# A list of operations that begins at slot 10 of the first layer instead of slot 28

## The chip, the cores and the metric

The kernel runs on one core of one Trainium2 chip. The metric is the device time of one execution in microseconds, from the first to the last thing that the program does there. Five engines work beside each other, each through its own instructions in order: TensorE (PE in the profile, its weight loads PEld), VectorE (DVE), ScalarE (ACT), GpSimd (POOL) and SyncE (SP), which here issues every transfer between the device memory and the core's SBUF. TensorE writes its results into eight banks of PSUM.

## The reference

Three steps, all in float32. First a retention (an attention without softmax, with a decay): for 4 batches, 8 heads, 576 positions and 64 values a head, the scores q k^T / 8 are multiplied by gamma^(i - j) for j <= i and by 0 otherwise, and by v. The result is one matrix x of 2304 tokens by 512 values. Then two layers of the same shape:

```
h = x @ w_in            # 512 -> 2048
g = h * cos(h)          # second layer: 0 for h <= -1, h for h >= 1, (h + 1)^2 / 4 between
x = g @ w_out           # 2048 -> 512
```

## The kernel before

**Numbers in two parts.** Every operand of a product is kept as a high and a low part (fp32r), and a product is made of three: high by high, the weight's low by high, the weight's high by low. The weights come as raw 64-bit words and are converted on the chip.

**Tokens and slots.** The tokens stand in five blocks, the first of 256 and four of 512 (`BLOCKS`, line 25). The 2048 hidden values stand in 16 parts. A slot is one block with one part; `slots` (from line 556) lists the 80 of them, the first two blocks interleaved (slots 0 to 31), then blocks 2, 3 and 4 with 16 slots each. A slot of block 0 is narrow (256 columns), the others are wide (512). Slot s has a first product (`mm1`, step m: h = x w_in, 12 matmuls), a chain that makes g of h, and a second product (`mm2`, step M, 12 matmuls into banks that gather the output). The chain is, in order: h, a copy out of PSUM (tile hs; blocks 0 and 1 alone), a (turns, ScalarE), A (rounded, VectorE), b (cosine, two steps of ScalarE), C (times h, VectorE), g (the high part gh, ScalarE), G (the low part gl, GpSimd). The first product has two PSUM banks in turn, so that of slot s + 2 needs the copy of slot s. The second product of a slot stands two slots behind its first (`LAG` = 2).

**The first layer's weights** (wi0 to wi15, wo0 to wo15) are converted on the way (`Conversion`): each needs a raw load and, for most, the same words again shifted by two bytes (tiles raw and rsh, two homes of each); then X (ScalarE, reads raw), C (VectorE, reads rsh), W (VectorE, two steps), O (ScalarE, the high part) and M (VectorE, the low part). The converted wi are also stored (`store1`, wd) and loaded again for blocks 2 to 4.

**The second layer's weights** are prepared in the background from slot 28 (`bg0`) on, in 32 pieces (`piece`): a raw load, X, W and two more steps, a high part and a low part in a home of the wi ring (tile cw), stores of it; each second piece also makes sums of two pieces, which are rounded (tile tw) and stored in four parts. The second layer loads all of these as tiles w from wq and wv; its first product of all (bkT<-xc,w) reads the first of them.

**What sets the order.** The opening is a list written by hand (`OPENING`), kept as it is on every engine. Then, before the change, a plain loop issues slots 10 to 27, whose order the compiler's scheduler chooses. From slot 28 on the order comes from a planner: `op` notes for each operation its engine, a cost (`COST`), a place in time, what it reads and what it writes, and `listed` goes through them with one clock for each engine: of the operations that are ready it takes the one whose place is earliest; TensorE's stand in the order noted; one of SP can't start before its place. The order found is kept on every engine, and what the planner took for time is not used on the chip. The second layer's list follows behind the first layer's on every engine, SP too.

Of the kernel before, what the change touches and what calls it, by code (L numbers as in the profile page):

```python
# [14 lines left out]
ALU = mybir.AluOpType  # L15
# [35 lines left out]
E1 = 5.75  # L51
PACE = 9.0
BG_AT = 0.0
BEHIND = 8.0
LATS = (0.12, 0.2)
COST = dict(turn=0.58, psum1=0.68, cos=1.3, copy4=0.65, low4=0.69, low2=0.42, copy2=0.42, copy8=1.06, low8=1.23, masks=1.12, state=1.1, high=0.75, scores=1.0, w8=0.86, nothing=0.02, PE=1.04, mm2=2.72, psum=0.556, wide=0.96, copy=0.85, square=0.9, evac=0.68, pool=2.15, load=0.06)
# [53 lines left out]
a:8 b:7 A:8 g:6 W:wo4 m:9 b:8 G:6 M:5 h:9 M:wo4 a:9 C:7 A:9 M:6 g:7 C:8 O:wo4 G:7 g:8 b:9 G:8 M:7 C:9 g:9 G:9 M:8  # L110
low:8 store:5
# [4 lines left out]
def retention_moe_kernel(ctx: ExitStack, tc: tile.TileContext, qk, kv, win1, wout1, win2, wout2, ktab, out):  # L116
# [656 lines left out]
    for _ in range(2):  # L773
        load_raw(0, *queue.pop(0))
# [98 lines left out]
    def listed(lat):  # L873
        waits = [len(o[4]) for o in ops]
        users = [[] for _ in ops]
        for n, o in enumerate(ops):
            for x, lands in o[4]:
                users[x].append((n, lands))
        ready = [o[2] if o[0] == "SP" or not o[4] else 0.0 for o in ops]
        free = dict(PE=0.0, ACT=0.0, DVE=0.0, POOL=0.0, SP=-60.0)  # L880
        queue = {e: {n for n, o in enumerate(ops) if o[0] == e and (e == "PE" or not waits[n])} for e in free}
        order = []
        while len(order) < len(ops):
            best = None
            for e, ns in queue.items():
                if e == "PE":
                    n = min(ns, default=None)
                    if n is None or waits[n]:
                        continue
                elif ns:  # L890
                    t1 = min(max(free[e], ready[n]) for n in ns) + 0.15
                    n = min((n for n in ns if max(free[e], ready[n]) <= t1), key=lambda n: (ops[n][2], n))
                else:
                    continue
                t = max(free[e], ready[n])
                if best is None or t < best[0]:
                    best = t, n
            t, n = best
            e, cost = ops[n][:2]
            queue[e].remove(n)  # L900
            free[e] = t + cost
            order.append((t, n))
            for u, lands in users[n]:
                ready[u] = max(ready[u], t + cost + (0.0 if not lands or ops[u][0] == e else 6.0 if e == "SP" else lat))
                waits[u] -= 1
                if not waits[u] and ops[u][0] != "PE":
                    queue[ops[u][0]].add(u)
        return order

    loop_end = bg0  # L910
    for s in range(bg0):
        if s == 24:
            by_hand[0] = 0
        steps_of(s, "m")
        if s >= 1:
            steps_of(s - 1, "CgG")
        steps_of(s, "haA")

        todo = [x for x in jobs.get(s, []) if x not in opened]
        begun = [begin(0, *x) for x in todo]  # L920
        for x in todo:
            begun.pop(0).rest(home1(*x))
            if queue:
                load_raw(0, *queue.pop(0))
        for x in todo:
            if x[0] == 0:
                store1(x[1])
        if s >= LAG:
            steps_of(s - LAG, "M")
            evac(s - LAG)  # L930
        steps_of(s, "b")

    def when(s):
        return (s - bg0) * E1

    def first_layer_ops():
        LOW = "DVE"
# [6 lines left out]
        def retention(i, k, g, e):  # L944
# [16 lines left out]
            def at_load():  # L961
                op("SP", "load", t0 - 17, lambda: load(0), (), (q,))
                op("SP", "load", t0 - 16, lambda: load(1), (), (v,))
# [8 lines left out]
            def at_attend():  # L972
                op("PE", "scores", t0 + E1, go("attend", *(() if last else ("state",))), (q, v, ("T",), ("R",)), banks)
                if CHUNKS[i][1] == 0:
                    op("ACT", "high", t0 + E1 + 1, go("add_state"), banks, (("T",),))
                elif not last:
                    op("DVE", "state", t0 + E1 + 1, go("add_state"), banks, (("T",),))
                op("ACT", "high", t0 + E1 + 2, go("high"), banks, (("xh", l),))
                opened_by.append(op("DVE", "w8", t0 + E1 + 3, go("low"), (*banks, ("xh", l)), (("xl", l),)))
# [20 lines left out]
        def wi_place(s):  # L1000
            return ("cw", 1) if s == bg0 else ("wi", s % 3)

        def chain(s, which="aAbCgG"):
            b, h, t, j = when(s), bank_of(s), ("t", s % 3), (N1 - 1 - s) % (LAG + 1)
            hi, lo = ("gh", j), ("gl", j)
            for x in which:
                eng, cost, pos, reads, writes = dict(
                    a=("ACT", "turn", 2.8, (h,), (t,)), A=("DVE", "psum1", 3.7, (h,), (t,)), b=("ACT", "cos", 5.0, (), (t,)),
                    C=("DVE", "psum1", 6.5, (h,), (t,)), g=("ACT", "copy4", 8.0, (t,), (hi,)), G=(LOW, "low4", 9.0, (t, hi), (lo,)))[x]
                op(eng, cost, b + pos, lambda x=x: steps_of(s, x), reads, writes)  # L1010

        def second(s):
            l, c = slots[s]
            j = (N1 - 1 - s) % (LAG + 1)
            op("PE", "mm2", 0, lambda: steps_of(s, "M"), (("gh", j), ("gl", j)), keys_y(l) if c in (0, NC - 1) else ())
            if c == NC - 1:
                o, n = BLOCKS[l]
                per = 512 // n
                for e, y in enumerate(keys_y(l)):
                    eng = ("ACT", "DVE")[e >= 2]  # L1020
                    opened_by.append(op(eng, "copy4", when(s + LAG) - 5, lambda e=e, eng=eng: evac(s, only=e, eng=eng), (y,)))


        dp = PACE
        prev = {}

        def piece(j):
            i, c = bg[j]
            p = j * dp + BG_AT
            raw, X, W, cw = ("raw", j % 3), ("X", j % 2), ("W", j % 2), ("cw", j % 2)  # L1030
# [33 lines left out]
            op("SP", "load", p - 10, lambda: load_raw(1, i, c), (), (raw,))  # L1064
# [4 lines left out]
            op("DVE", "low4", p + 3, joined, (X, W), (("V", 0), ("V", 1)) if not two_of_it else (v,))  # L1069
# [4 lines left out]
            for a, b in pieces:  # L1074
                op("SP", "load", p + 6, lambda a=a, b=b: store(a, b), (cw,))
# [33 lines left out]
            for k, a in enumerate(((5, 4, 7, 6), (5, 7, 4, 6))[i]):  # L1109
                op("SP", "load", p + 9, lambda k=k, a=a: store_sum(k, a), (("tw",),))  # L1110

        chain(bg0 - 1, "CgG")
        done_pieces = 0
        for s in range(bg0, N1):
            for fn in plan.pop(2 * s, []):
                fn()
            if s >= pos_of[2, 0]:
                op("SP", "load", when(s) - 13, lambda s=s: load_wi(slots[s][1]), (), (wi_place(s),))
            l = slots[s][0]
            op("PE", "mm2", 0, lambda s=s: steps_of(s, "m"), (wi_place(s), ("xh", l), ("xl", l)), (bank_of(s),))  # L1120
# [3 lines left out]
            second(s - LAG)  # L1124
            while done_pieces < len(bg) and done_pieces * dp + BG_AT <= when(s + 1):
# [339 lines left out]
```

## Time and profile before

| | us |
|---|---|
| three runs | 820.22, 818.06, 821.0 (median 820.22) |
| the profiled execution | 818.65 |
| its span, first to last instruction | 816.9 |
| TensorE busy | 805.4 |
| VectorE busy | 635.1 |
| ScalarE busy | 542.7 |
| GpSimd busy | 126.2 |

The opening takes about the first 77 us of the span; slots 10 to 27 come next; the list of the first layer goes on to 456 us; the second layer takes the rest. In the profile L133 is the line through which the ordered part of the program issues, so the tiles' names tell what an operation is: h and hs belong to the first product, gh and gl to the chain's end, bky, bkS and bkO to the second product, X, W, C, raw, rsh, wi, wo to a conversion, cw, tw and V to the second layer's pieces. A matmul's duration includes the filling of the array, so that the starts of two neighbours lie closer than a duration.

### The profile page before, as it was taken

Reading aid. Unit: us, or ns where it says so; the run is one execution under the profiler, and the core shown is the slowest. Engines: PE = TensorE matmul, PEld = TensorE weight load, DVE = VectorE, ACT = ScalarE, POOL = GpSimd, SP = SyncE. Lnnn points to the kernel's source line nnn. Section 1 sums busy time; section 2 is a strip of 40 time slices with the busy share of each in tenths; the row PEclk is TensorE's granted clock in tenths of the full one; section 3 lists DMA queues with packets and bytes.
Section 4 is the critical chain, followed back from the end, with each engine's and each line's share of the span. In section 5 each row is a group of like instructions: output and inputs, shape, how many; then the busy total and the mean of one; then the engine's idle time right before and its main releaser. Section 6 shows DMA issues by size and latency. Waiting matters only on the chain.

```text
span 816.9 us, 14708 instructions
## 1 busy us (share of the span) xinstructions
PE 805.4 (99%) x5549; PEld 728.2 (89%) x5550; DVE 635.1 (78%) x956; ACT 542.7 (66%) x890; POOL 126.2 (15%) x99
## 2 busy tenths in 40 slices
PE   8999999999999999999999999999999999999997
PEld 6888789888878888888888899999999999999997
DVE  7988878697898877887896377886777885974675
ACT  4778788765556656666765578786666786576671
POOL 2333222222122222232232100000000000000000
PEclk9999999999999999999999999999999999999999
DMA  9997999399777998688976699888899888888883
GB/s 358 396 388 281 357 321 336 133 354 346 272 276 260 338 327 275 228 303 279 340 238 230 203 336 293 291 250 253 254 333 325 251 254 255 272 307 253 254 256 127
DMA packets 78006, 232.92 MB, mean 285 GB/s; under 512 B 8304, under 2 KB 15088, under 8 KB 77936
## 3 DMA queue, kind: packets, MB, share of 16 engines
q1 hardware_dynamic: 77936, 231.98, 82.7%
q8 instruction: 44, 0.72, 0.3%
q14 instruction: 26, 0.21, 0.1%
HBM read 184.76 MB, written 47.19 MB: 284 GB/s over the span
## 4 chain that ended last, share of the span: by engine, by line
PE 90%; DMA 4%; DVE 2%; ACT 2%; issue 1%; SPq 0%; POOL 0%; DVEq 0%; ACTq 0%; POOLq 0%
PE bkT L133 42%; PE bky L133 21%; PE h L133 19%; PE bkS L133 4%; PE bkO L133 4%; DMA rsh<-in_wout_dram 2%; DMA qkv<-in_qk_dram 1%; PE h L580 1%; DMA qkv<-in_kv_dram 1%; DMA raw<-in_wout_dram 1%; ACT t L133 1%; DVE t L133 0%; ACT gh L133 0%; DVE wo L133 0%; DVE X L133 0%
## 5 line engine op out<-in xcount | busy, mean ns | idle before, releaser
L133 PE MATMUL h<-xhl,wi 128*128 128x512 f32 (+1 forms) x816 | 180.7, 370 | 2.2 <-ACT hs L133 1.8
L133 PE MATMUL bkT<-xc,w 128*128 128x384 f32 x1008 | 179.0, 335 | 0.0
L133 PEld LDWEIGHTS bkT<-xc,w 128*128 128x128 f32 x1008 | 175.2, 188 | 0.5 <-ACT bkT L133 0.3
L133 PE MATMUL bkT<-gh,w 128*128 128x384 f32 x672 | 170.8, 335 | 0.3 <-ACT bkT L133 0.3
L133 PEld LDWEIGHTS h<-xhl,wi 128*128 128x128 f32 x816 | 142.1, 189 | 29.3 <-ACT hs L133 2.0
L133 PE MATMUL bky<-gh,wo 128*128 128x512 f32 x504 | 155.2, 395 | 0.0
L133 POOL TENSOR_TENSOR gl<-t,gh 128x512 fp32r<-128x512 f32 (+1 forms) x76 | 103.7, 1366 | 300.4 <-ACT gh L133 278.4
L133 PEld LDWEIGHTS bkT<-gh,w 128*128 128x128 f32 x672 | 121.2, 188 | 0.6 <-ACT bkT L133 0.6
L133 PE MATMUL bkT<-gl,w 128*128 128x384 f32 x336 | 112.3, 334 | 0.0
L133 PEld LDWEIGHTS bky<-gh,wo 128*128 128x128 f32 x504 | 94.5, 190 | 19.8 <-issue 0.5
L133 ACT ACTIVATE t<-t 128x512 f32<-128x512 f32 (+1 forms) x152 | 89.3, 590 | 34.0 <-DVE t L133 31.9
L133 PE MATMUL bky<-gl,wo 128*128 128x512 f32 x252 | 95.6, 390 | 0.0
L133 DVE SCALAR_TENSOR_TENSOR t<-t,h 128x512 f32<-128x512 f32 x88 | 60.1, 683 | 35.1 <-ACT t L133 35.1
L133 PEld LDWEIGHTS bkT<-gl,w 128*128 128x128 f32 x336 | 63.1, 188 | 0.0
L133 ACT ACTIVATE gh<-t 128x512 fp32r<-128x512 f32 (+1 forms) x76 | 44.7, 588 | 26.0 <-DVE t L133 25.9
L133 PEld LDWEIGHTS bky<-gl,wo 128*128 128x128 f32 x252 | 47.2, 188 | 9.9
L133 DVE TENSOR_TENSOR gl<-a,gh 128x768 fp32r<-128x768 f32 x48 | 45.2, 953 | 13.8 <-ACT gh L133 13.8
L133 ACT ACTIVATE t<-h 128x512 f32<-128x512 f32 x44 | 26.2, 595 | 43.4 <-PE h L133 43.4
L133 DVE SCALAR_TENSOR_TENSOR a<-bkT,a 128x768 f32<-128x768 f32 x36 | 34.4, 955 | 23.3 <-ACT a L133 22.7
L133 DVE TENSOR_TENSOR a<-bkT,a 128x768 f32<-128x768 f32 (+1 forms) x46 | 43.0, 937 | 11.0 <-PE bkT L133 11.0
L133 ACT ACTIVATE X<-raw 128x512 f32<-128x512 f32 x61 | 40.5, 666 | 11.5 <-DMA raw<-in_win_dram 7.1
L133 ACT ACTIVATE gh<-a 128x768 fp32r<-128x768 f32 x48 | 40.2, 837 | 9.0 <-PE bkT L133 8.4
(159 smaller groups left out, 1180.6 us busy)
## 6 DMA issues: line engine op xcount, KB each, us to landing
w<-wq SPq DMA_DIRECT2D x84, 512.0 KB, 4.6
w<-wv SPq DMA_DIRECT2D x84, 512.0 KB, 4.5
wi<-wd SPq DMA_DIRECT2D x48, 512.0 KB, 5.6
raw<-in_win_dram SPq DMA_DIRECT2D x32, 512.0 KB, 5.8
raw<-in_wout_dram SPq DMA_DIRECT2D x32, 512.0 KB, 5.9
qkv<-in_qk_dram SPq DMA_DIRECT2D x16, 512.0 KB, 6.9
qkv<-in_kv_dram SPq DMA_DIRECT2D x16, 512.0 KB, 8.0
wd<-wi SPq DMA_DIRECT2D x16, 512.0 KB, 6.2
```

The source lines that it names most:

```text
L133: ins = fn(*args, **kw)
L580: lastpe[0] = PE.matmul(hp[s][:, :n], w[:, a, kb, :], x[b][:, kb, :], start=(i == 0), stop=(i == 3 * KB - 1))
```

## The change

- `OPENING` (line 94): the conversions of wi6 and wo5 stand in its last lines, and `store:5` is taken out.
- The two raw loads behind the opening, and the loop over slots up to 27, are gone. The first layer's list begins at the first slot whose first product is not in the opening, slot 10, and holds the rest of the conversions (`converted`), their raw loads (a pair is one operation of SP) and the stores.
- The planner's clock (`when`) is no longer 5.75 us a slot: `begins` adds 2.72 us for each wide product and 1.45 for each narrow one, and 1.15 for each retention step (`held`).
- The planner counts transfers one after another: 1.3 us for 512 KB, and 2 us more to land.
- The cost table (not shown) tells wide steps from narrow ones: on ScalarE 0.65 and 0.42 for a copy, 0.6 and 0.42 for a turn, 1.3 and 0.86 for a cosine.
- Eight wide slots (`LATER`) have their second product three slots behind; the lows of the same slots (`LOW_DVE`) go to VectorE.
- `PACE` goes from 9.0 to 9.3 and `BEHIND` from 8 to 14; pieces and reloaded wi are noted as users of five homes of one ring (w5).

```
-E1 = 5.75
-PACE = 9.0
+PACE = 9.3
+CONV_AT = 9.0
+STORES = (5, 6)
+LATER = (10, 12, 15, 17, 19, 21, 24, 26)
+LOW_DVE = (10, 12, 15, 17, 19, 21, 24, 26)
 BG_AT = 0.0
-BEHIND = 8.0
+BEHIND = 14.0
...
-a:8 b:7 A:8 g:6 W:wo4 m:9 b:8 G:6 M:5 h:9 M:wo4 a:9 C:7 A:9 M:6 g:7 C:8 O:wo4 G:7 g:8 b:9 G:8 M:7 C:9 g:9 G:9 M:8
-low:8 store:5
+a:8 b:7 A:8 g:6 W:wo4 m:9 b:8 G:6 M:5 h:9 M:wo4 a:9 C:7 A:9 M:6 g:7 X:wi6 C:8 C:wi6 O:wo4 G:7 g:8 W:wi6 b:9 G:8 M:7
+O:wi6 C:9 M:wi6 g:9 X:wo5 G:9 C:wo5 W:wo5 M:8 low:8 M:wo5 O:wo5
...
-        G.tensor_tensor(out=gl[s], in0=u, in1=f(gh[s]), op=ALU.subtract)
+        (V if s in LOW_DVE else G).tensor_tensor(out=gl[s], in0=u, in1=f(gh[s]), op=ALU.subtract)
...
-    for _ in range(2):
-        load_raw(0, *queue.pop(0))
...
+            lands_at = t + cost + 6.0
+            if e == "SP" and cost > COST["load"]:
+                sent[0] = max(sent[0], t) + {COST["one"]: 1.3, COST["two"]: 2.6, COST["halfof"]: 0.65}[cost]
+                lands_at = max(sent[0] + 2.0, t + 3.2)
...
-    loop_end = bg0
-    for s in range(bg0):
-        if s == 24:
-            by_hand[0] = 0
-        steps_of(s, "m")
-        if s >= 1:
-            steps_of(s - 1, "CgG")
-        steps_of(s, "haA")
-        todo = [x for x in jobs.get(s, []) if x not in opened]
-        begun = [begin(0, *x) for x in todo]
-        for x in todo:
-            begun.pop(0).rest(home1(*x))
-            if queue:
-                load_raw(0, *queue.pop(0))
-        for x in todo:
-            if x[0] == 0:
-                store1(x[1])
-        if s >= LAG:
-            steps_of(s - LAG, "M")
-            evac(s - LAG)
-        steps_of(s, "b")
+    by_hand[0] = 1
+    first_slot = min(s for s in range(N1) if ("m", s) not in taken)
+    begins = {first_slot: 0.0}
+    held = {}
+    for l in range(3, NBLK):
+        s0, s1 = pos_of[l - 1, 0] + 1, pos_of[l - 1, NC - 1] - 1
+        for j in range(len(members[l])):
+            g = int(2 * s0 + j * 2 * (s1 - s0) / len(members[l]))
+            for x in (g // 2, g // 2 + 1):
+                held[x] = held.get(x, 0.0) + 1.15
+    def lag(s):
+        return LAG + (s in LATER)
+    for s in range(first_slot, N1):
+        both = [s] + [x for x in range(s - LAG - 1, s) if x + lag(x) == s and ("M", x) not in taken]
+        begins[s + 1] = begins[s] + sum(2.72 if BLOCKS[slots[x][0]][1] == 512 else 1.45 for x in both) + held.get(s, 0.0)
+    for s in range(first_slot - 1, -1, -1):
+        begins[s] = begins[s + 1] - 4.0
+    begins[N1 + 1] = begins[N1] + 5.44
     def when(s):
-        return (s - bg0) * E1
+        s0 = int(s)
+        return begins[s0] + (s - s0) * (begins[s0 + 1] - begins[s0])
...
         def wi_place(s):
-            return ("cw", 1) if s == bg0 else ("wi", s % 3)
-        def chain(s, which="aAbCgG"):
-            b, h, t, j = when(s), bank_of(s), ("t", s % 3), (N1 - 1 - s) % (LAG + 1)
+            return ("w5", slots[s][1] % 5) if s < pos_of[2, 0] else ("w5", (3, 4, 0)[(s - pos_of[2, 0]) % 3])
...
+            d, h, t, j = when(min(s + lag(s), N1)) + 2.72, bank_of(s), ("t", s % 3), (N1 - 1 - s) % (LAG + 1)
...
+                    h=("ACT", "copy" + z, -9.0, (h,), (src,)),
+                    a=("ACT", "turn" + z, -8.0, (src,), (t,)), A=("DVE", "low" + z, -7.0, (src,), (t,)), b=("ACT", "cos" + z, -6.0, (), (t,)),
...
+                    C=("DVE", "low" + z, -4.3, (src,), (t,)), g=("ACT", "copy" + z, -3.2, (t,), (hi,)), G=(*low_on(s), -2.2, (t, hi), (lo,)))[x]
...
+        def converted(n, x):
+            i, c = x
+            need = when(pos_of[0, c] + LAG * i) + 2.7 * i
+            at_home = ([("wo", 12), ("wo", 13)], [("wo", 8), ("wo", 9)], [("wo", 10), ("wo", 11)])[{(0, 7): 0, (1, 5): 1, (0, 6): 2}[x]] if x in loaded else None
+            raw_count[0] += at_home is None
+            raw, rsh = at_home or (("raw", raw_count[0] % 2), ("rsh", raw_count[0] % 2))
+            X, W, C = ("X", n % 2), ("W", n % 2), ("C", n % 2)
+            to = (("w5", c % 5), ("wo", c))[i]
+            cb = {}
+            if x in queue:
+                op("SP", "two", need - 24, lambda: load_raw(0, i, c), (), (raw, rsh))
...
+            p = need - CONV_AT
+            op("ACT", "copy4", p, lambda: conversion().X(), (raw,), (X,))
+            op("DVE", "low2", p + 1, lambda: conversion().C(), (rsh,), (C,))
+            op("DVE", "w8", p + 2, lambda: cb[0].W(), (), (X, W))
+            op("ACT", "copy4", p + 3, high, (W,), (to,))
+            op("DVE", "low4", p + 4, lambda: cb[0].M(), (C, X), (to,))
+            if i == 0:
+                op("SP", "one", p + 8, lambda: store1(c), (to,))
...
-            p = j * dp + BG_AT
-            raw, X, W, cw = ("raw", j % 3), ("X", j % 2), ("W", j % 2), ("cw", j % 2)
+            p = T28 + j * dp + BG_AT
+            k3 = (turn0 + j) % 3
+            raw, X, W, cw = (("raw", 0), ("raw", 1), ("rsh", 0))[k3], ("X", j % 2), ("W", j % 2), ("w5", 1 + j % 2)
...
-            op("SP", "load", p - 10, lambda: load_raw(1, i, c), (), (raw,))
+            op("SP", "one", p - 10, lambda: load_raw(1, i, c), (), (raw,))
             p += BEHIND
...
-                op("SP", "load", p + 6, lambda a=a, b=b: store(a, b), (cw,))
+                op("SP", "halfof", p + 6, lambda a=a, b=b: store(a, b), (cw,))
...
-                op("SP", "load", p + 9, lambda k=k, a=a: store_sum(k, a), (("tw",),))
-        chain(bg0 - 1, "CgG")
-        done_pieces = 0
-        for s in range(bg0, N1):
+                op("SP", "halfof", p + 9, lambda k=k, a=a: store_sum(k, a), (("tw",),))
...
+        work = [(s, x) for s in sorted(jobs) for x in jobs[s] if x not in opened]
+        done_pieces = done_convs = 0
+        chain(first_slot - 1)
+        for c in STORES:
+            op("SP", "one", 2.0 + 4.0 * (c - 5), lambda c=c: store1(c), (("w5", c % 5),))
+        while work[done_convs][0] < first_slot:
+            converted(done_convs, work[done_convs][1])
+            done_convs += 1
...
+            if s - LAG - 1 in LATER:
+                second(s - LAG - 1)
...
+            if s - LAG not in LATER:
+                second(s - LAG)
+            while done_convs < len(work) and work[done_convs][0] <= s:
+                converted(done_convs, work[done_convs][1])
+                done_convs += 1
```

## Rows read from the trace of the kernel before

**Rows 1.** The page: span, TensorE's busy time and the granted clock in 40 slices.
```profile
span 816.9 us, 14708 instructions
...
PE 805.4 (99%) x5549; PEld 728.2 (89%) x5550; DVE 635.1 (78%) x956; ACT 542.7 (66%) x890; POOL 126.2 (15%) x99
...
PEclk9999999999999999999999999999999999999999
```

**Rows 2.** Stretches of 5 us: busy us of each engine, clock, DMA share, GB/s.
```profile
60.00:65.00 5.00, 5.00 (x29) 4.36 (x28) 4.77 (x10) 4.82 (x12) 2.41 (x2) 1.00 1.03 419
...
75.00:80.00 5.00, 5.00 (x25) 4.17 (x24) 4.97 (x12) 3.20 (x6) 1.24 (x1) 1.00 0.26 107
...
85.00:90.00 5.00, 3.21 (x25) 2.92 (x24) 3.50 (x8) 4.71 (x11) 0.72 (x1) 0.99 1.01 398
90.00:95.00 5.00, 5.00 (x20) 4.16 (x19) 4.97 (x10) 4.94 (x13) 1.71 (x2) 0.67 1.04 405
```

**Rows 3.** Two later stages, columns as in rows 2.
```profile
95.00:150.00 55.00, 55.00 (x330) 49.05 (x329) 43.95 (x80) 43.76 (x92) 15.38 (x14) 1.00 0.91 323
...
346.00:456.00 110.00, 110.00 (x487) 91.08 (x486) 84.99 (x132) 70.11 (x116) 31.13 (x20) 1.00 0.81 281
```

**Rows 4.** TensorE in order of time: start, us, tiles, shape, count, idle before.
```profile
67.16 1.60 PE L133 MATMUL h<-xhl,wi 128*128 128x256 f32 x12
...
74.68 0.39 PE L133 MATMUL bky<-gl,wo 128*128 128x512 f32 x1
...
76.95 4.32 PE L133 MATMUL h<-xhl,wi 128*128 128x512 f32 x24
...
88.68 1.96 PE L133 MATMUL h<-xhl,wi 128*128 128x256 f32 x12 [1.79 <-ACT hs L133]
90.43 3.35 PE L133 MATMUL bky<-gh,wo 128*128 128x512 f32 x8
...
99.80 2.00 PE L133 MATMUL bky<-gh,wo 128*128 128x512 f32 x8
```

**Rows 5.** The chain of waits from 76 to 92 us: start, us, what.
```profile
79.86 5.41 DMA raw<-in_wout_dram
...
85.29 0.68 ACT X L133
...
88.15 0.49 ACT hs L133
```

**Rows 6.** GpSimd in order of time, 70 to 76 us.
```profile
71.84 1.29 POOL L133 TENSOR_TENSOR gl<-t,gh 128x512 fp32r<-128x512 f32 x1 [0.26 <-POOL gl L133]
```

**Rows 7.** SP's issues in order of time: start, us from first to last, count.
```profile
57.79 7.63 SPq L133 DMA_DIRECT2D wd<-wi  x3
65.47 0.43 SPq L133 DMA_DIRECT2D raw<-in_wout_dram  x1
```

**Rows 8.** DMA issues from 60 to 140 us: KB each, us to landing.
```profile
wd<-wi SPq DMA_DIRECT2D x10, 512.0 KB, 5.7
raw<-in_wout_dram SPq DMA_DIRECT2D x10, 512.0 KB, 5.5
rsh<-in_wout_dram SPq DMA_DIRECT2D x10, 511.8 KB, 5.8
```

**Rows 9.** VectorE in order of time, 439 to 451 us.
```profile
439.68 0.69 DVE L133 TENSOR_TENSOR cw<-V,cw 128x512 fp32r<-128x512 f32 x1 [1.29 <-ACT cw L133]
```

**Rows 10.** SP's issues in order of time, 427 to 461 us.
```profile
445.42 1.79 SPq L133 DMA_DIRECT2D wv<-tw  x4
447.30 13.91 SPq L133 DMA_DIRECT2D w<-wq  x6
```

**Rows 11.** DMA issues from 447.2 to 447.6 us: KB, us to landing.
```profile
w<-wq SPq DMA_DIRECT2D x1, 512.0 KB, 4.3
```

**Rows 12.** TensorE in order of time, 452.5 to 461 us.
```profile
455.85 2.24 PE L133 MATMUL bkT<-xc,w 128*128 128x384 f32 x12
```

**Rows 13.** ScalarE in order of time, 438 to 452 us.
```profile
443.08 1.05 ACT L133 ACTIVATE tw<-V 128x1024 fp32r<-128x1024 f32 x1
```

More of the change, by code (lines that the diff above doesn't have):

```diff
@@ L50 @@
 XPOS = (-17, -20, -17.5, -4.4, -13, -4.5, -3.2)
-E1 = 5.75
-PACE = 9.0
+PACE = 9.3
[3 more added lines that the diff above has]
+LOW_DVE = (10, 12, 15, 17, 19, 21, 24, 26)
 BG_AT = 0.0
-BEHIND = 8.0
+BEHIND = 14.0
 LATS = (0.12, 0.2)
-COST = dict(turn=0.58, psum1=0.68, cos=1.3, copy4=0.65, low4=0.69, low2=0.42, copy2=0.42, copy8=1.06, low8=1.23, masks=1.12, state=1.1, high=0.75, scores=1.0, w8=0.86, nothing=0.02, PE=1.04, mm2=2.72, psum=0.556, wide=0.96, copy=0.85, square=0.9, evac=0.68, pool=2.15, load=0.06)
+COST = dict(turn4=0.6, turn2=0.42, cos4=1.3, cos2=0.86, mm1=1.45, one=0.3, halfof=0.31, two=0.6, copy4=0.65, pool4=1.45, pool2=0.9, psum4=0.68, low4=0.69, low2=0.42, copy2=0.42, copy8=1.06, low8=1.23, masks=1.12, state=1.1, high=0.75, scores=1.0, w8=0.86, nothing=0.02, PE=1.04, mm2=2.72, psum=0.556, wide=0.96, copy=0.85, square=0.9, evac=0.68, pool=2.15, load=0.06)
 LAG = 2
@@ L961, in at_load @@
             def at_load():
[L962 to L963 removed]
+                op("SP", "one", t0 - 17, lambda: load(0), (), (q,))
+                op("SP", "one", t0 - 16, lambda: load(1), (), (v,))
                 op("DVE", "low4", t0 - 6, lambda: CH[i].decay_q(V), (), (q,))
@@ L1020, in second, with conversion, high @@
                     eng = ("ACT", "DVE")[e >= 2]
-                    opened_by.append(op(eng, "copy4", when(s + LAG) - 5, lambda e=e, eng=eng: evac(s, only=e, eng=eng), (y,)))
+                    opened_by.append(op(eng, "copy4", when(s + lag(s)) - 5, lambda e=e, eng=eng: evac(s, only=e, eng=eng), (y,), (next_st(),)))
+        raw_count = [0]
+        def converted(n, x):
[9 more added lines that the diff above has]
+                op("SP", "two", need - 24, lambda: load_raw(0, i, c), (), (raw, rsh))
+            def conversion():
+                if not cb:
+                    cb[0] = Conversion(0, i, c)
+                return cb[0]
+            def high():
+                cb[0].o = home1(i, c)
+                cb[0].O()
+            p = need - CONV_AT
[6 more added lines that the diff above has]
+                op("SP", "one", p + 8, lambda: store1(c), (to,))
         dp = PACE
+        T28 = when(bg0)
+        turn0 = turn[0]
         prev = {}
@@ L1123, in first_layer_ops @@
                 fn()
-            second(s - LAG)
-            while done_pieces < len(bg) and done_pieces * dp + BG_AT <= when(s + 1):
+            if s - LAG not in LATER:
[3 more added lines that the diff above has]
+                done_convs += 1
+            while s >= bg0 and done_pieces < len(bg) and T28 + done_pieces * dp + BG_AT <= when(s + 1):
                 piece(done_pieces)
```

45 lines of the change are left out of this document (31 added, 14 removed).

## The prediction

> **What bounds the kernel now.** I read the page first: TensorE is busy for 805.4 of 816.9 us and its granted clock is full in every slice [rows 1]. The products themselves are not changed, so I looked next at where TensorE is late: the stretches of 5 us around the place of the change [rows 2], the longer stages behind it [rows 3], and the order of matmuls on TensorE [rows 4]. From 95 to 150 us and from 346 to 456 us it is busy for the whole stage at full clock, while VectorE and ScalarE are busy for 44 of the 55 us, so no step there is waited for. One place is left: from 85 to 90 us TensorE works 3.21 of 5 us, and from 90 to 95 us its granted clock is 0.67. In the order of matmuls that is one idle stretch of 1.79 us, ended by ScalarE's copy hs, and slow products behind it. The chain of waits [rows 5] says why the copy was late: ScalarE stood in front of a conversion's first step (X) for a raw weight that was issued at 79.86 and took 5.41 us to come; the copy hs, which frees a bank of PSUM, was queued behind that X.
>
> This gives the most that the change can win behind 60 us: 1.79 us of idle, and the slow products. Twelve products of 256 columns took 1.96 against 1.60 us, eight of 512 took 3.35 against 2.00 [rows 4]: 0.36 + 1.35 = 1.7. Together 3.5 us, 0.43%. The granted clock of 0.67 is a mixture of the two levels, 2.4 and 1.2 GHz; ahead of it TensorE had been idle for 1.79 us.
>
> **The change part by part.**
>
> *Two conversions more in the opening (wi6, wo5).* The same steps ran directly behind the opening before, so they are moved and not added. X:wi6 now stands ahead of O:wo4 and g:8 on ScalarE and costs g:8 at most one X, 0.68 us [rows 5]. GpSimd's low of slot 8 started at 71.84 and lasts 1.29 [rows 6]; TensorE first reads it at 74.68 [rows 4]. That is 1.55 us of cover for 0.68: cost 0. Without cover it would be 0.68 and a part of the slow clock.
>
> *Store 5 out of the opening, raw loads and stores as operations of the list.* SP stood in three stores for 7.63 us until the raw pair for wo6 could go at 65.47 [rows 7]. It can go earlier now, but DMA is full at that time (419 GB/s from 60 to 65 us [rows 2]), so what lands first changes and not how much: 0.
>
> *Slots 10 to 27 by the list.* The late copy goes if the list puts X behind hs. It does: the planner counts a raw pair as 2.6 us of transfer and 2 us more, so it has the pair for wo6 at 4.6 us behind slot 10's first product, and the copy of slot 10 is ready at 2.72 + 0.2. What is late next is the raw data themselves. A raw home is free when X and C have read it. X of wo6 now stands behind the copies of slots 10 and 11: 2.72 + 1.45 us of products, 0.42 for the copy, 0.65 for X, with the latencies 5.5 us behind slot 10's start at 76.95 [rows 4]. So the pair for wo7 goes at 82.5 instead of 79.86 [rows 5]. From there 16 pairs of 1.05 MB and 11 stores of 0.52 MB remain [rows 8], 22.5 MB. The last conversion's use is slot 27's second product; ahead of it are 18 wide products of 2.72 and 20 narrow ones of 1.45, 78 us, so it comes at 155, and its conversion starts 9 us earlier: the loads have from 82.5 to 146, 63.5 us. From 95 to 150 us DMA moved 323 GB/s at a share of 0.91 [rows 3], which is 355 at a full share: 63.4 us, no slack. At 419 GB/s it is 54 us, 10 us of slack. The planner counts 403 (512 KB in 1.3 us), near the better end. So the old stall goes (-3.5), and new ones cost between 0 and twice an old one (7.0, rival two). Nearest is the row of 95 to 150 us, the same traffic, where 0.91 did not stop TensorE; I take 1.0.
> The Trainium skill (DMA: Bandwidth & Descriptors, Specifications) gives some 358 GB/s as one core's share of the HBM's rate. The stretch from 95 to 150 us agrees with it (355); that from 60 to 65 us, 419 GB/s, does not. By that figure alone the loads would take 63 of the 63.5 us, and rival two would be as likely as the forecast.
>
> *Second products three slots behind, lows on VectorE.* Eight slots get one slot more between their chain and its use. Their lows leave GpSimd, where one takes 1.29 us [rows 6], for VectorE, where such a step takes 0.69 [rows 9]. VectorE has 11 us free in 55 [rows 3] and gets 8 x 0.69 = 5.5. Cost 0, and 0.69 for each that finds VectorE busy, if the slot more did not cover it.
>
> *The pace of the second layer's weights (PACE 9.3, BEHIND 14).* Nothing waits for these 32 pieces until the first layer ends, but SP issues their last stores ahead of the first weight that the second layer loads. Before, that last group of stores went at 445.42 and the first weight at 447.30 [rows 10], with 4.3 us to land [rows 11]: 451.6, while TensorE wanted it at 455.85 [rows 12]. There were 4.2 us to spare.
> How far does the group move? In the planner a store does not go before its place in time, and a home is not written again before its store has landed. Before: piece 29's sums may go at 29 x 9 + 8 + 9 = 278 us behind slot 28 and land 6 later, so piece 31's sums are rounded from 284 on, and the layer ends at 52 x 5.75 = 299: 15 ahead. In the trace they were rounded at 443.08 [rows 13], 12.8 ahead: the planner's time holds on the chip to 2 us, since every engine keeps the order that it writes. After: 29 x 9.3 + 14 + 9 = 292.7, 4.1 to land, 296.8; the layer ends at 2.72 + 6.89 + 50 x 5.44 + 18 x 1.15 = 302.3: 5.5 ahead. So the group comes 9.5 us later against the layer's end. The planner counts a retention step at 1.0 where its clock has 1.15: 18 x 0.15 = 2.7, so the shift may be 12.2. On the other hand its own TensorE can fall behind its clock in slots 10 to 27, where it has 19 conversions of 1.3 us, 8 wide chains of 3.2 and 10 narrow ones of 2.1 for ScalarE, 71 us in 69.8; that gives 1 to 5 us back. I take 9.5 - 2 = 7.5, and as ends 4.2 and 12.2. At 7.5 the first weight lands 7.5 - 4.2 = 3.3 us late, TensorE stands for it, since the first product of that layer is the next in its queue, and the clock falls as it did behind 1.79 us: 1.7 more. Cost 5.0; ends 0 and 12.2 - 4.2 + 1.7 = 9.7.
>
> *Sum.* The profiled execution took 818.65 us, 816.9 of it span. 818.65 - 3.5 + 1.0 + 5.0 = 821.15. The three other runs have a median of 820.22, all four a mean of 819.5, so I add 0.85: **822.0 us**, within what a measurement of this kernel can tell from no change (0.5% either way, 816.1 to 824.3).
>
> **The rivals.**
> One: the whole gain stays. The last stores keep ahead of TensorE and no load is late. For it: the first weight had 4.2 us to spare. Against: the place of the stores in the planner moved by twice as much. 818.65 - 3.5 + 0.85 = 816.0.
> Two, slower: ScalarE stands at X for raw data in slots 14 to 22, because the transfers run at 355 GB/s and the list is written for 403. Its price is an idle stretch like the old one with its slow clock, 3.5 us each time; it decides from two on, as the layer's end is paid besides: 818.65 - 3.5 + 7.0 + 5.0 + 0.85 = 828.0. For it: two raw homes, and the later start at 82.5. Against: TensorE did not stop at the same traffic from 95 to 150 us [rows 3], and a second product three slots behind forgives a late conversion.
> Three: the change doesn't do what it says. The idle stretch before 88.68 only moves to another copy behind another X, and the layer's end stays covered: 818.65 + 0.85 = 819.5.
>
> **How the numbers follow.** Forecast 0.45 (its own range 817 to 826.5), rival one 0.20, two 0.20, three 0.15. Under 816.1 lies half of rival one: 0.10. Over 824.3 lie a third of the forecast and all but 0.01 of rival two: 0.34. Between: 0.56. The range goes from rival one's lower half, 815.5, to rival two, 828.5.
>
> **What would show it.** The old stall: no idle stretch of TensorE between 85 and 95 us, clock 1.0 there. The loads: the pair for wo7 issued at 82 to 83 and a DMA share of 0.95 or more up to 145 us; ScalarE idle at an X behind a raw load, and TensorE idle behind that, would be rival two. The layer's end: the last group of wv stores within 5 us of the second layer's first product instead of 10.4, the first weight issued behind it, TensorE idle until that lands, and a granted clock under 1.0 behind the gap. If TensorE crosses that end without a gap, the shift was under 4.2 us, and the largest term of the sum is wrong; if it stands there for over 8 us, the planner gave nothing back.

## The result, and the profile after

The changed kernel took **831.94 us**, median of five runs (831.07 to 832.27), the kernel before 820.22 in the same comparison (817.12 to 821.0): a ratio of 1.015, interval 1.0127 to 1.0174. The forecast was 822.0 and its range ended at 828.5. So the kernel became slower by 1.5%, and by more than I had allowed for. A few executions of the experiments below took 1.4 to 3.4 times as long as the others of the same kernel; no time below counts them, and e1 and e9 have no profile because the profiled execution was one of them.

The page of the changed kernel: its span, the engines' busy time, the shares of the chain that ended last, and the group of the second layer's first kind of product (busy, mean ns, idle before and what ended it):
```profile
span 830.5 us, 14697 instructions
...
PE 810.3 (98%) x5550; PEld 729.7 (88%) x5550; DVE 635.2 (76%) x964; ACT 545.1 (66%) x894; POOL 114.2 (14%) x91
...
PE 84%; DMA 8%; DVE 4%; ACT 3%; issue 1%; SPq 1%; DVEq 0%; ACTq 0%; POOL 0%; POOLq 0%
...
L136 PE MATMUL bkT<-xc,w 128*128 128x384 f32 x1008 | 180.5, 337 | 3.5 <-DMA w<-wq 3.5
```
Beside [rows 1] TensorE's busy time is 4.9 us longer and the span 13.6: the new time is idle time and slow products, not work. Three marks in TensorE's order say where it went in. Slot 10 begins at 79.59 (76.95 in [rows 4]), slot 28 at 159.35 (150.45 before), the second layer's first product at 468.42 (455.85 in [rows 12]):
```profile
79.59 1.07 PE L136 MATMUL h<-xhl,wi 128*128 128x512 f32 x4
...
159.35 1.32 PE L136 MATMUL h<-xhl,wi 128*128 128x512 f32 x5
...
468.42 3.73 PE L136 MATMUL bkT<-xc,w 128*128 128x384 f32 x12 [3.51 <-DMA w<-wq]
```
Opening: +2.6. Slots 10 to 27: 79.8 us for 73.5, +6.3. From slot 28 to the layer's end: +3.7. Behind it: +1.0, most of it slow products. Together 13.6.

The stretches of [rows 2] and [rows 3] in the changed kernel, and three more (same columns: PE, PEld, DVE, ACT, POOL, clock, DMA share, GB/s):
```profile
80.00:85.00 5.00, 5.00 (x34) 4.57 (x34) 4.18 (x8) 3.25 (x7) 0.73 (x1) 1.00 0.00 0
85.00:90.00 5.00, 5.00 (x30) 4.26 (x30) 4.93 (x13) 4.94 (x12) 0.06 (x1) 1.00 0.67 192
90.00:95.00 5.00, 5.00 (x34) 4.55 (x34) 3.22 (x8) 4.01 (x9) 0.96 (x1) 1.00 1.00 400
95.00:150.00 55.00, 48.71 (x271) 41.61 (x270) 39.85 (x81) 41.79 (x87) 5.91 (x7) 0.97 0.93 337
...
105.00:110.00 5.00, 1.58 (x10) 1.38 (x11) 4.66 (x10) 4.26 (x9) 0.77 (x1) 0.97 0.98 349
110.00:115.00 5.00, 5.00 (x20) 4.22 (x20) 3.01 (x8) 2.77 (x6) 0.82 (x1) 0.69 0.92 351
...
465.00:470.00 5.00, 1.58 (x5) 1.61 (x6) 0.66 (x1) 0.63 (x1) 1.26 (x1) 0.81 1.02 354
```
The old stall is gone: TensorE is busy throughout 85 to 95 us, at full clock. But the stage of 95 to 150 us, in which TensorE had not stopped once, now holds 6.3 us of idle, with clock 0.69 behind the longest piece of it. VectorE is busy for 39.85 of these 55 us and yet is the engine that is late. Its waits from 77 to 165 us (total, times, longest), with TensorE's longest behind them:
```profile
DVE C L136 <- DMA rsh<-in_wout_dram: 9.6, 9, 1.5
DVE C L136 <- DMA rsh<-in_win_dram: 5.9, 6, 1.7
...
ACT X L136 <- DMA raw<-in_wout_dram: 2.0, 3, 1.4
ACT X L136 <- DMA raw<-in_win_dram: 0.9, 2, 0.5
...
PE bkS L136 <- ACT gh L136: 3.7, 2, 3.2
```
A conversion reads two raw tiles: X (ScalarE) the first of the pair, C (VectorE) the second, rsh. Here 15 of the list's 19 C's stood in front of a tile that had not landed, for 15.5 us; before, one did, for 0.7. How a wait at C reaches TensorE is seen around the longest stall, all engines in order of time:
```profile
102.00 0.61 ACT L136 ACTIVATE t<-hs 128x512 f32<-128x512 f32 x1
...
103.21 1.60 PE L136 MATMUL h<-xhl,wi 128*128 128x256 f32 x12
...
104.48 0.43 DVE L136 TENSOR_SCALAR C<-rsh 128x512 int32<-128x512 int32 x1 [1.05 <-DMA rsh<-in_win_dram]
104.82 1.02 DVE L136 SCALAR_TENSOR_TENSOR t<-t,hs 128x512 f32<-128x512 f32 x2
...
105.54 1.29 ACT L136 ACTIVATE t<-t 128x512 f32<-128x512 f32 x2 [1.25 <-DVE t L136]
...
106.74 0.66 ACT L136 ACTIVATE X<-raw 128x512 f32<-128x512 f32 x1
...
107.30 0.36 ACT L136 ACTIVATE hs<-h 128x256 f32<-128x256 f32 x1
...
107.56 0.40 ACT L136 ACTIVATE gh<-t 128x256 fp32r<-128x256 f32 x1
...
108.02 0.50 PE L136 MATMUL bkS<-gh,wo 128*128 128x256 f32 x2 [3.20 <-ACT gh L136]
```
VectorE's step t could have run once the turn of 102.00 was done, at 102.61. But a C stands ahead of it and waits for rsh until 104.48, so t comes late, so ScalarE's cosine starts only at 105.54 after 1.25 us of waiting, and behind the cosine stand X, hs and at last the copy gh that TensorE needs. One late tile on VectorE makes both engines late, because each keeps the order that the list wrote.

The chain of waits that leads to that C goes from one load of rsh through a C to the next:
```profile
87.65 8.95 DMA rsh<-in_win_dram
...
96.62 0.43 DVE C L136
...
97.08 7.31 DMA rsh<-in_win_dram
...
104.48 0.44 DVE C L136
```
A home of rsh is loaded again only when the C before has read it, and here 15 C's run as soon as their tile has landed. So the two homes are a loop of their own. That this loop alone sets the time is not what the runs show: e14 below has such loads on its chain too, sends the same 16 pairs in 54.8 us (60.3 here, first to last issue of rsh), and TensorE hardly stops. A third pair of homes was not tried.

At the layer's end, ScalarE, SP and TensorE:
```profile
459.41 1.04 ACT L136 ACTIVATE tw<-V 128x1024 fp32r<-128x1024 f32 x1
...
461.74 1.78 SPq L136 DMA_DIRECT2D wv<-tw  x4
...
463.62 11.65 SPq L136 DMA_DIRECT2D w<-wq  x6
```
In [rows 13] and [rows 10] these were 443.08, 445.42 and 447.30. Against the layer's end they moved from 12.8 us ahead (sums) to 5.5 (459.41 to 464.9, where the product would have begun without its 3.51 us of idle).

### The profile page after: what moved, and what is told of

Read it like the earlier page. It is cut to its first block, busy times and chain, and to the rows that moved or that the text cites. A ratio compares the mean times of both kernels' runs of the same rounds, so it can differ in the third digit from the quotient of the medians.

```text
span 830.5 us, 14697 instructions
## 1 busy us (share of the span) xinstructions
PE 810.3 (98%) x5550; PEld 729.7 (88%) x5550; DVE 635.2 (76%) x964; ACT 545.1 (66%) x894; POOL 114.2 (14%) x91
## 4 chain that ended last, share of the span: by engine, by line
PE 84%; DMA 8%; DVE 4%; ACT 3%; issue 1%; SPq 1%; DVEq 0%; ACTq 0%; POOL 0%; POOLq 0%
PE bkT L136 42%; PE bky L136 18%; PE h L136 17%; DMA rsh<-in_win_dram 5%; PE bkS L136 3%; PE bkO L136 3%; DMA rsh<-in_wout_dram 1%; ACT t L136 1%; DMA qkv<-in_kv_dram 1%; DVE t L136 1%; DVE C L136 1%; DMA w<-wq 1%; SPq L136 1%; DVE X L136 0%; DVE W L136 0%
## 5 line engine op out<-in xcount | busy, mean ns | idle before, releaser
L136 PE MATMUL h<-xhl,wi 128*128 128x512 f32 (+1 forms) x864 | 189.1, 370 | 1.0 <-DVE wi L136 1.0
L136 PEld LDWEIGHTS h<-xhl,wi 128*128 128x128 f32 x864 | 150.0, 190 | 28.9 <-DVE wi L136 1.2
L136 PE MATMUL bky<-gh,wo 128*128 128x512 f32 x512 | 159.0, 392 | 0.0
L136 POOL TENSOR_TENSOR gl<-t,gh 128x512 fp32r<-128x512 f32 (+1 forms) x72 | 96.3, 1337 | 332.3 <-ACT gh L136 307.7
L136 ACT ACTIVATE t<-t 128x512 f32<-128x512 f32 (+1 forms) x160 | 93.5, 588 | 39.1 <-DVE t L136 36.4
L136 PE MATMUL bky<-gl,wo 128*128 128x512 f32 x256 | 100.3, 392 | 1.3 <-DVE gl L136 1.3
L136 DVE SCALAR_TENSOR_TENSOR t<-t,h 128x512 f32<-128x512 f32 x80 | 54.7, 683 | 29.0 <-ACT t L136 28.6
L136 ACT ACTIVATE X<-raw 128x512 f32<-128x512 f32 x64 | 42.6, 666 | 35.6 <-DMA raw<-in_wout_dram 19.5
L136 ACT ACTIVATE gh<-t 128x512 fp32r<-128x512 f32 (+1 forms) x80 | 46.5, 584 | 28.8 <-DVE t L136 28.4
L136 DVE TENSOR_TENSOR gl<-a,gh 128x768 fp32r<-128x768 f32 x48 | 45.2, 954 | 13.5 <-ACT gh L136 13.5
L136 ACT ACTIVATE a<-bkT,half 128x768 f32<-128x768 f32 x36 | 32.4, 901 | 17.7 <-PE bkT L136 17.4
```

Source lines behind the costliest of these rows:

```text
L136: ins = fn(*args, **kw)
```

## The experiments

"Slots" is the time from slot 10's first product to slot 28's (73.5 before, 79.8 after), "C" the sum of VectorE's waits at C for raw tiles from 77 to 165 us, "end" TensorE's idle time in front of the second layer's first product. These three come from one profiled execution of each kernel. Times are medians; ratios are to the kernel before on the same chip (817.6 to 818.5 us in these comparisons, 820.22 in that of the changed kernel, so that a gain on the changed kernel is some 2 us smaller by the ratios than by the times).

| kernel | us | ratio, interval | slots | C | end |
|---|---|---|---|---|---|
| changed | 831.94 | 1.015 (1.0127 to 1.0174) | 79.8 | 15.5 | 3.5 |
| e1 pace back | 825.77 | 1.0103 (1.0073 to 1.0133) | | | |
| e2 pairs start earlier | 832.05 | 1.0166 (1.0143 to 1.0189) | 81.9 | 18.4 | 3.1 |
| e3 landing +4 | 824.97 | 1.008 (1.006 to 1.01) | 74.2 | 6.2 | 3.2 |
| e4 two slots, lows on GpSimd | 826.39 | 1.009 (1.0065 to 1.0115) | 76.5 | 7.5 | 1.9 |
| e5 before, new pace alone | 820.26 | 1.0023 (1.0008 to 1.0038) | 73.1 | 0.7 | 1.1 |
| e6 before, new opening alone | 817.72 | 0.9992 (0.9979 to 1.0004) | 70.5 | 0 | 0 |
| e7 pace back, landing +4 | 822.66 | 1.0043 (1.0026 to 1.006) | 75.7 | 3.6 | 0 |
| e8 e7 and e4 | 820.68 | 1.0025 (1.0014 to 1.0036) | 73.2 | 2.6 | 0 |
| e9 lows on GpSimd | 833.43 | 1.0182 (1.0158 to 1.0207) | | | |
| e10 two slots | 823.13 | 1.0067 (1.0043 to 1.0091) | 74.9 | 9.8 | 1.4 |
| e11 landing +3 | 824.96 | 1.009 (1.0074 to 1.0105) | 73.2 | 8.8 | 3.1 |
| e12 two slots, pace back, landing +3 | 823.8 | 1.0077 (1.0065 to 1.0089) | 78.5 | 10.3 | 0 |
| e13 due as with two slots | 826.28 | 1.0106 (1.0092 to 1.0121) | 75.2 | 11.0 | 3.4 |
| e14 as e12, landing +4 | 819.72 | 1.0023 (1.001 to 1.0037) | 72.0 | 6.1 | 0 |
| e15 as e12, landing +2 | 821.98 | 1.006 (1.0046 to 1.0075) | 75.0 | 8.2 | 0 |

**The pace: e1 and e5.** e1 is the changed kernel with
```
-PACE = 9.3     -BEHIND = 14.0
+PACE = 9.0     +BEHIND = 8.0
```


> The changed kernel (831.9 us) with PACE 9.0 and BEHIND 8 as before, nothing else. Its trace has TensorE idle for 3.5 us at the end of the first layer, in front of the first weight of the second, and 1.7 us of slow clock behind. Theory A (the stores of the last pieces were moved behind the layer's end): that stretch goes, nothing else moves, 826 to 828 us, and the last wv stores go 9 us earlier against the layer's end. Rival (the stretch is a consequence of the lateness of slots 10 to 27, which pushes all that follows): it stays, 831 to 833.

It took 825.77 (825.29, 825.77 and 828.65), 6.2 less than the changed kernel, or 3.8 by the ratios: 0.2 under theory A's 826 to 828, and far from the rival's 831 to 833. That the stretch itself goes can't be seen in e1, which has no profile. It is seen in two pairs of kernels that differ by the pace alone: from e3 to e7 the idle time at the end falls from 3.2 us to 0, and from e10 to e15 from 1.4 to 0. e5 is the other direction, the kernel before with PACE 9.3 and BEHIND 14.0 alone.


> The kernel before with PACE 9.3 and BEHIND 14 and nothing else of the change. Theory A (these two numbers alone move the last stores behind the second layer's first weight): in the planner of before, piece 31's sums may be rounded from 29 x 9.3 + 14 + 9 + 6 = 298.7 us behind slot 28 instead of 284, 14.7 later, so TensorE stands some 14.7 - 4.2 = 10.5 us for the weight and loses 1.7 more to the slow clock: 828 to 832. If the stall is limited by something else to the 5 us that the changed kernel shows: 824 to 826. Rival (the layer's end of the changed kernel is late for another reason, its own list): no change, 817 to 821.

820.26: slower than the kernel before by a ratio of 1.0023, far less than the 828 of theory A and inside the rival's range. SP and TensorE at the layer's end of e5:
```profile
453.43 1.87 SPq L133 DMA_DIRECT2D w<-wq  x4
...
458.86 2.33 SPq L133 DMA_DIRECT2D wv<-tw  x4
...
457.71 2.32 PE L133 MATMUL bkT<-xc,w 128*128 128x384 f32 x12 [1.11 <-DMA w<-wq]
```
The last sums did move (rounded at 456.54 instead of 443.08, 13.5 us for the 14.7 computed), but four of the second layer's weight loads stand ahead of their stores in SP's order here, so the first weight went 6.1 us later than before and not 13. The planner's shift came out, which the rival did not have; that the stores stay ahead of the weights in SP's order, my premise, does not hold for every list. In the changed kernel it does. Why they passed each other in e5 was not settled. Over all profiles the pace decides cleanly whether there is a stall: the eight with 9.3 and 14 stand for 1.1 to 3.5 us at the layer's end, the five with the list and 9.0 and 8.0 for none.

**The start of the pairs: e2.** The planner is told that the pairs loaded ahead of the list are no longer on the way:
```
-        sent = [0.0]
+        sent = [-60.0]
```


> The changed kernel, and its planner counts the raw pairs of wo6 and wi8, which are issued at the end of the opening, as landed when its list begins (its transfer clock starts at -60 instead of 0). Theory B (late start: with only two raw homes the conversions run no faster than TensorE needs them, so the first pair's issue at 85.15 instead of 79.43 us is never made up): X of wo6 runs some 4 us earlier, the pair for wo7 goes at 80 to 82, TensorE's idle time in slots 10 to 27 falls from 6 to 8 us with its slow clock to under 2, 822 to 826 us. Rival C (the planner counts a pair as landed 2 us too early each time, so VectorE stands at every C): the 15 waits of C for rsh stay, 830 to 832.

The pair for wo7 went at 79.20 instead of 85.15, and nothing was won: 832.05, and C waits 18.4 us, as theory C has it. The 5 us without any transfer (80 to 85 us above) look like the culprit in the changed kernel and are not: e3 and e14 have the same zero there.

**The landing: e3, e11, and with the pace e7.**
```
-                lands_at = max(sent[0] + 2.0, t + 3.2)
+                lands_at = max(sent[0] + 4.0, t + 5.2)
```


> The changed kernel, and its planner counts every transfer as landing 2 us later. Theory C (the landing is counted 2 us too early, so that X and C stand too early in the order and what is behind them waits): VectorE's waits at C fall from 15.4 us to under 4, TensorE's idle time in slots 10 to 27 mostly goes, 823 to 826. Theory B (late start): X of wo6 stands 2 us later still, the first pair goes later, idle time stays or grows, 831 to 836.

824.97, C waits 6.2 (not under 4), slots 74.2: theory C's range for the time, and not theory B's. The edit counts every transfer so, stores too. e11 has 3.0 and 4.2 in this line.


> The changed kernel with a pair of raw loads counted as landed 3 us behind its transfer (2 in the changed kernel, 4 in the kernel that gained 7 us). Theory C (the list puts VectorE's C in front of data that are not there yet): the waits at C fall from 15.4 us to some 10 and the time to 827 to 830, between the two. Rival (any other list would have been as good, the gain came from a lucky order): no order among the three, 831 or more, or under 825.

The same time as e3; its C waits lie between (8.8). So theory C's range, 827 to 830, was missed, and 824.96 lies at the edge of the rival's "under 825": by the times alone a lucky order is not excluded. The traces show the order itself. Ahead of each of the list's 19 C's VectorE runs on average 2.5 chain steps (t) more in e3 than in the changed kernel, 1.0 more in e11 and 0.6 fewer in e2; the waits at C are 6.2, 8.8 and 18.4 us, with 15.5 in the changed kernel. So a landing that is counted later does put C behind more chain steps, and C then waits less.

Two microseconds is what the planner counts behind a pair's transfer, 4.6 with the transfer; on the chip the second tile of a pair landed 6.5 to 6.8 us behind its own issue in the changed kernel (median, 77 to 165 us) and 6.5 to 6.7 in e14. So a tile does not land sooner behind its issue in the better list; its C is only written later.
The Trainium skill (DMA: Bandwidth & Descriptors, Anatomy of one DMA) gives some 2 us and the bytes at 436 GB/s for one transfer, a fit made for GpSimd's queue; the planner's count has that form. By that fit a tile of 512 KB would take an estimated 3.2 us; the median above is beyond it by some 3 us. The tile issued just ahead, most often a pair still on its way and at times a store were under way besides; what each of them adds was not measured.

e7 is e3 with PACE 9.0 and BEHIND 8.0.


> The changed kernel with both mended: PACE 9.0 and BEHIND 8.0 again, and a pair of raw loads counted as landed 4 us behind its transfer instead of 2. If the two costs are separate they add: 831.9 - 4.7 - 7.1 = 820 (818.5 to 821.5), no stall at the layer's end and under 7 us of VectorE's waits at C for raw data from 77 to 165 us. If they share something (the earlier stores hide behind the late list): 822 to 825.

822.66, not the 820 of separate costs, and within the second case. The end is free (0), but slots take 75.7, 1.5 more than in e3, and there is a slow clock that e3 had not.

**The slot more and the lows: e4, e9, e10, e8.** e4 takes both back, e9 the lows, e10 the slot more:
```
-LATER = (10, 12, 15, 17, 19, 21, 24, 26)       e4, e10:  +LATER = ()
-LOW_DVE = (10, 12, 15, 17, 19, 21, 24, 26)     e4, e9:   +LOW_DVE = ()
```


> The changed kernel with no slot three behind and all lows on GpSimd again (LATER and LOW_DVE empty). Theory D (the eight lows on VectorE, and the second products that stand later, make VectorE late): 824 to 828. Theories B and C: the slot more only helped, since late conversions are now waited for a slot earlier, 832 to 840.

> The changed kernel with all lows on GpSimd again, the eight second products still three slots behind. Theory D1 (of the 5.3 us that lag and lows on VectorE cost together, the lows cost nearly all, since on VectorE they stand behind its waits at C for raw data): 826 to 828, with PE waiting under 1 us for a low. Rival D2 (the slot more costs it, by moving the products and with them the homes of the weights): 830 to 833.

> The changed kernel with every second product two slots behind, the eight lows still on VectorE. Theory D1 (the lows cost it): without the slot more they have less time, so 832 to 836. Rival D2 (the slot more costs it): 826 to 828. If both give some 2.5 us, 829 to 830 in this and in the run before.

826.39, 833.43 and 823.13. e4 lies in theory D's range and not in that of theories B and C, by which the slot more only helped. Theory D1 falls: with the lows back on GpSimd alone the kernel is no faster. D2 had the right sign, but two slots alone give more than it said: 8.8 us, 6.8 by the ratios. By the profiles 4.9 of it lie in the slots (79.8 to 74.9) and 2.5 ahead of slot 10, and the rest at the layer's end and its slow clock, where the idle is 2.1 us shorter. Between e4 and e10 the lows on VectorE seem a gain of 3.3, but the intervals of the two ratios overlap.
e8 is e7 with both lists empty.


> As the kernel with both mended, and the lows back on GpSimd with every second product two slots behind. Theory D (lows on VectorE stand behind its waits at C, 5 us in the changed kernel) has little left to give once C waits little: 816 to 820, and under the kernel before only if the new list then stalls less than the old one (3.5 us). Rival (the slot more is needed when conversions come late): 821 to 824.

820.68, between theory D's range (to 820) and the rival's (from 821); a ratio of 1.0025 behind the kernel before.

**How the slot more costs: e13.** TensorE keeps its order; only the planner's places for the chains of these slots are those of two slots:
```
-            d, h, t, j = when(min(s + lag(s), N1)) + 2.72, ...
+            d, h, t, j = when(min(s + LAG, N1)) + 2.72, ...
```


> The changed kernel with its eight products still three slots behind, but the chains of those slots given the planner's places of two slots behind. Theory L2 (the slot more costs because the planner gives those chains later places, so that conversion steps stand ahead of chain steps on VectorE and ScalarE): 823 to 827. Rival L1 (TensorE's own order costs: two products without a second product between them, then two second products at once): 830 to 833.

826.28, slots 75.2: theory L2's range, and as good there as e10 with its 74.9. So TensorE's own order costs nothing that shows, and the runs point to the later place of those chains (5.7 us by the times, 3.6 by the ratios). That it costs by letting conversion steps stand ahead of chain steps is not shown: ahead of a C there are on average 0.6 chain steps more than in the changed kernel in e13, but none more in e10. The layer's end is as late as in the changed kernel (3.4). One more home of gh and gl, which would test the homes, was not tried.

**The opening alone: e6.** The kernel before with the new opening; stores 5 and 6 at its end, the loop of slots 10 to 27 as it was:
```
-... C:9 g:9 G:9 M:8 low:8 store:5
+... X:wi6 C:8 C:wi6 O:wo4 G:7 g:8 W:wi6 b:9 G:8 M:7
+O:wi6 C:9 M:wi6 g:9 X:wo5 G:9 C:wo5 W:wo5 M:8 low:8 M:wo5 O:wo5 store:5 store:6
```


> The kernel before with the two conversions wi6 and wo5 inside the opening at the places of the changed kernel; the stores of 5 and 6 stand at the end of the opening, and the written loop of slots 10 to 27 is left. My step 'cost 0' says 817 to 821. Theory E (these conversions make the steps of slot 8 and 9 late, and the 2 us that TensorE lost more ahead of 78 us in the changed kernel come from there): 821 to 823, with the gap of about 1.2 us near 58 us.

817.72, no change (0.9992). But its slots take 70.5 us, 3.0 less than before, and the stretches of the old stall are nearly full, the first with a DMA share of 0.99 where the kernel before had 0.85:
```profile
80.00:85.00 5.00, 5.00 (x35) 4.63 (x34) 3.61 (x8) 3.83 (x9) 0.00 (x0) 1.00 0.99 369
85.00:90.00 5.00, 4.62 (x27) 3.87 (x26) 3.21 (x9) 4.70 (x11) 1.67 (x2) 1.00 1.03 410
```
ScalarE's longest wait at X for a raw tile is 0.6 us here, 1.6 before. The raw tile for wo7 is issued later than before (81.55 instead of 79.86), but its X stands later still: it starts at 88.89, 7.3 us behind the issue instead of 5.4, and does not wait. So the opening is enough to remove the old stall; the list of slots 10 to 27 was not needed for it. That the time does not show the 3.0 is mostly slot 10's start, 77.9 in this profile and 77.0 in that of before.

**Together: e15, e12, e14.** Two slots, lows on VectorE, PACE 9.0, BEHIND 8.0; the landing +2, +3 and +4.


> The changed kernel with two slots everywhere and PACE 9.0 and BEHIND 8.0, the landing as in the changed kernel (2 us). The layer's end is free: 823.1 less 1.7 is 821.4 (820 to 822.5). If the counted landing costs nothing without the slot more, this equals the kernels with 3 and 4 us.

> The changed kernel with the three costs found so far mended: every second product two slots behind (the eight lows stay on VectorE), PACE 9.0 and BEHIND 8.0, a raw pair counted as landed 3 us behind its transfer. If the lag is a cost of its own: two slots alone gave 823.1, the layer's end there still stood for 1.7 us and slots 10 to 27 for 5.3; with the end free and some 2 us less in the slots, 817 to 820, level with the kernel before. If the lag only made the early conversions worse, so that the mended landing already holds its gain: 820 to 823.

> As the kernel with three costs mended, the pair counted as landed 4 us behind its transfer. If the counted landing matters once the lag is gone: 816 to 819; if 3 us is already enough: the same as that kernel within 1.5 us.

821.98, 823.8, 819.72: not in the order of the landing. e15 is in its range; e12 is above both of its own, and e14 lies between its first case and its second. e12 has two slow clocks and 78.5 us in its slots, more than either neighbour. So a list is uncertain by 3 to 4 us, since each number re-sorts the whole of it, and a difference of that size between two lists says little about the one number that was changed. The order once written repeats: e10 and e15 have the same C's behind the same number of chain steps, and 74.9 and 75.0 us in the slots. The best, e14, needs 72.0 us for the slots, at the same bytes and with the same empty stretch:
```profile
80.00:85.00 5.00, 5.00 (x35) 4.63 (x34) 2.29 (x5) 3.68 (x7) 0.00 (x0) 1.00 0.00 0
...
78.00:150.00 72.00, 71.57 (x421) 62.34 (x420) 59.39 (x119) 59.09 (x124) 7.91 (x10) 1.00 0.87 316
```
No kernel here beats the one before by more than its interval; e6 is level with it, e14 0.23% behind.

## Why the prediction was wrong

**The step that failed** is the term "new ones cost between 0 and twice an old one (7.0, rival two) ... I take 1.0". The slots became 6.3 us longer although the old stall of 3.5 [rows 2, 4] went, so the new stalls cost some 9.8. The row that I took it from, 95 to 150 us of the kernel before, says that this traffic can be lived with by the order of that loop. It says nothing of another order, and the order was what changed. The pair for wo7 was no surprise: it went at 85.15 instead of the 82.5 computed, but 5.6 us behind slot 10's start as computed (5.5). I had asked whether the bytes come in time and whether X stands ahead of a late tile. The engine that stood was VectorE, at C, and the sum in the planner that put it there (2.6 us of transfer and 2 more) I had read, quoted, and used as proof that X comes behind hs, without holding its 4.6 us against the 5.8 us that [rows 8] show for rsh. That this count is what put C there is shown by the orders of e2, e3 and e11; how much of the 9.8 it is, is not clear to better than the 3 to 4 us between lists.

**"Second products three slots behind, lows on VectorE: cost 0"** was half right. The lows on VectorE cost nothing that shows (e9). The slot more cost 4.9 us in the slots, part of the same 9.8, as e10 has it, and e13 points to the chains' later places; by what wait stays open.

**Rival two** had the sign and the place, and 828.0 was the nearest number. Its mechanism holds in part: DMA is nearly full from 90 to 115 us, at shares of 0.92 to 1.02 and 349 to 405 GB/s. But the rate did not decide, since e14 moves the same bytes from the same late start with slots of 72.0 us, and ScalarE's waits at X are 2.9 us against 15.5 at C. Over the changed kernel and the eleven variants of its list that have a profile, the most waiting at C goes with the longest slots (18.4 us and 81.9, 15.5 and 79.8); among the other ten there is no clear order (3.6 and 75.7 in e7, 6.1 and 72.0 in e14, 10.3 and 78.5 in e12).

**The layer's end (5.0)** was right in kind and size: 3.51 us of idle for the 3.3 computed, and the slow products behind it (1.5 for 1.7). The sums moved 7.3 us against the layer's end for the 7.5 taken. e7, e8, e12, e14 and e15 have no stall there with the pace of before. e5 shows that the size depends on SP's order as well.

**The old stall (-3.5)** went, as predicted. Whether X's place behind hs did it, the reason given, stays open: e6 removes it without the list.

**The opening (0):** slot 10 began 2.6 us later in the profile of the changed kernel. In the twelve profiles of kernels with the new opening and the list it began at 77.1 to 79.6, in the three without the list at 77.0 to 77.9. Perhaps 1 us is the change's, the rest differs from run to run.

**Sum of the miss:** 831.94 - 822.0 = 9.9; the slots 8.8 (9.8 for 1.0) and the opening 2.6 (for 0), less 0.3 at the layer's end (4.7 for 5.0), less the 0.85 that was added for the median, less the 0.3 by which the profiled execution is above its median.

## What to carry to other kernels

When an order written by a planner takes the place of one that ran well, a row of the old order bounds nothing: take the planner's assumed landing of each load and hold it against the measured median of that load in the same stretch, for every tile that an operation reads, not only the first. An in-order engine that is busy for 40 of 55 us can still be the one that is late, if a step that waits for a transfer stands ahead of the chain. Before crediting a large rewrite with the stall that it removes, try its smallest part alone.

## What was not expected of the hardware

The same idle stretch of TensorE is followed by the slow clock in one run and not in another. In e3 and in e7, which ran on different chips, it stands for 1.50 us in front of the same narrow second product, for ScalarE's wo; a shorter one follows, of 0.69 us in e3 and 0.31 in e7. The ten microseconds around it in e3 (clock in the third column from the right):
```profile
140.00:145.00 5.00, 2.98 (x18) 2.57 (x19) 3.73 (x9) 4.55 (x10) 0.88 (x1) 1.00 0.93 331
145.00:150.00 5.00, 5.00 (x29) 4.39 (x28) 3.07 (x7) 3.11 (x7) 0.28 (x1) 1.00 0.93 347
```
and in e7:
```profile
140.00:145.00 5.00, 3.19 (x21) 2.79 (x20) 4.29 (x10) 3.92 (x10) 0.73 (x1) 0.91 0.95 320
145.00:150.00 5.00, 5.00 (x23) 4.17 (x23) 1.98 (x4) 1.47 (x4) 0.97 (x1) 0.75 0.99 359
```
At the layer's end 1.11 us (e5) and 1.44 us (e10) of idle kept the full clock (1.00 in the stretches of 5 us around them), 1.87 us (e4) did not (0.87 and 0.79). So a sum of stalls of this length needs an end with the slow clock's 1.7 us in it and one without.

A step of VectorE that begins while a step of GpSimd runs can take much longer. The eight lows on VectorE in the changed kernel take 0.68 to 0.69 us, but for the two that began just behind a low of GpSimd, 1.22 and 1.23; TensorE waited behind both of them, 0.91 and 0.40 us. One of the two, and one that began alone:
```profile
97.97 0.80 POOL L136 TENSOR_TENSOR gl<-t,gh 128x256 fp32r<-128x256 f32 x1 [7.02 <-ACT gh L136]
98.10 1.22 DVE L136 TENSOR_TENSOR gl<-t,gh 128x512 fp32r<-128x512 f32 x1
...
111.88 0.69 DVE L136 TENSOR_TENSOR gl<-t,gh 128x512 fp32r<-128x512 f32 x1
```
None of the eight takes longer than 0.70 us in e10, e12, e14 and e15, the kernels with two slots and the lows on VectorE.
